# Unread matmuls from the first microsecond, k^T v copied by DMA, and seven taps of a convolution moved to ScalarE under a newly searched order

## The chip, the cores and the metric

The kernel runs on one core of a Trainium2 chip. A time is the device time of one execution in microseconds (us). A profile gives the span of one execution, some 2 us shorter than its time (203.0 against 204.8 us for the kernel before). Engine names: PE is TensorE's matmuls, PEld its weight loads, DVE is VectorE, ACT is ScalarE, POOL is GpSimd, SP is SyncE, which here issues most of the stores.

Some executions of half of the versions here ran some 4 us longer with a recorded PE clock near 0.98 of full. Where a few tenths of a microsecond matter I use only executions with a recorded clock of 0.994 or more, and call them full-clock runs; where all executions of a version are listed, the others are named. The recorded clock doesn't count time before the clock first rises (experiment 4), so a full-clock run can still have had a slow start.

## The reference, cut to what matters

Attention without a softmax, normalized per head, then a feed-forward layer with a gate from a convolution along the sequence. Eight batches, eight heads, 576 positions, head size 64; 512 model columns, 1024 inner columns; fp32 in and out.

```python
kv  = einsum('bhsd,bhse->bhde', k, v)            # 64 x 64 for each head
o   = einsum('bhsd,bhde->bhse', q, kv)
x   = o / sqrt(mean(o*o, axis=-1) + 1e-6) * g    # then heads side by side: 576 x 512
h   = maximum(x @ w_in, 0)                       # 576 x 1024
c   = sum_k conv_w[k] * shift(h, k - 1)          # three taps per column
out = (h * (1 / (1 + exp(-c)))) @ w_out          # 576 x 512
```

## The kernel before

The batches go in five groups (1, 1, 2, 2, 2). The program first lists some 700 operations, each a handful of instructions (a block of matmuls, an eviction, a store), and then sends them out in the sequence of a string that an offline search wrote. A letter after a number is the engine (`a` ScalarE, `d` VectorE), and `*n` puts n unread matmuls, called fillers below, in front of the operation:

```python
ORDER = """
    0 105 11 104 8 10 12 1 2 7 17 18a 9 19 20d 29 30a 24 25d 26*5 27 21 22 6 34 35d 31 32 103 23a 36
    37d 41*7 28d 38*3 40d 33d 4 42 43*6 44 108 109d 39 49 45 46 5 50 3 13 118*9 123 124a 51 53 119a
    106 107a 54 204 47 110*5 111 113 114a ...                                   # cut
"""

def fill(op, ps):                                # the unread matmuls
    for _ in range(op.fill):
        n = min(ps.shape[-1], 288)
        nc.tensor.matmul(ps[:, :n], ident, spread.rearrange("p c m -> p (c m)")[:, :n],
                         start=True, stop=True)
```

k^T v of two heads lands in one PSUM tile, one head on partitions 0 to 63, the other on 64 to 127. The product with q needs each on both halves of the partitions, so for seven of the eight batches it is evicted four times, each time half the partitions (`kv_out`). For the very first batch PE computes it twice (`kv_twice`).

```python
for i in range(2):
    for half in range(2):
        move(st["op"], dst[half * D:(half + 1) * D, :, i, :],
             src[i * D:(i + 1) * D, :, 0, :])
```

The outer taps of the convolution are multiplications of a tile by a column of weights, all on VectorE (`eng` could only be GpSimd otherwise), and output tiles have three buffers:

```python
eng.tensor_scalar_mul(cst["t"][:, f - f0, :], g.h[:, f, lo:lo + T], cw_rel[:, j, f:f + 1])
...
outp = pool("outp", 3)
```

For the last two groups the inverse norms go to DRAM and come back spread over partitions by eight DMAs, all in one operation of the order (`scatter`), issued on SP like the output stores.

Of the kernel before, what the change touches and what calls it, by code (L numbers as in the profile page):

```python
# [25 lines left out]
def _patch_pnc_remap() -> None:  # L26
# [45 lines left out]
KV_TWICE = (1, 0, 0, 0, 0)  # L72
TAPS = ("DVE",)
# [3 lines left out]
    0 105 11 104 8 10 12 1 2 7 17 18a 9 19 20d 29 30a 24 25d 26*5 27 21 22 6 34 35d 31 32 103 23a 36  # L77
    37d 41*7 28d 38*3 40d 33d 4 42 43*6 44 108 109d 39 49 45 46 5 50 3 13 118*9 123 124a 51 53 119a
    106 107a 54 204 47 110*5 111 113 114a 52 48 55 125 112d 56a 126 127d 14 203 202 68 69d 120 122d
    210 211d 121 220 115 116 59 117d 60d 128 129 130 57 58 77 64 207 215 65a 78a 73 74a 221d 131 132  # L80
    61 216d 62 225 226a 133 134 137 208 209a 138 206 135 82 136 83d 205 66 67 212 213 217 232 218
    364 214d 219d 233d 247 139 140a 222 224d 223 248d 227 237 238a 143 144a 242 243d 147 149 63 141
    75 228 142a 148 230 231d 362 79 229a 76 80 81 145 146a 363 15 234 249 250 236d 370 251a 70 239*4
    16 235 71 150 151 367 240 152 371d 153 155 86*3 87a 378 382 366 383d 244 245 156 365 72 379d 167
    252 168d 241d 253 254 374*2 375d 246a 84*3 85 163 164a 169 170a 88 165 154 89 255 157 158 166a
    171 90 259 256 368 369a 173 260 172 160 91 265 175 266 372 373 92d 93 267 268 174 376 377 388
    389a 384 385 396 397a 176 261*2 269 159 100 101a 161 179 516 515 270 262 177 257 386 380 97 387a
    381 390 392 258 178 283 180 393a 391 514 181 185 98d 400 401d 263 394 395 182 183 162 522 523d
    94 264 402 403 526 527d 184 519 398 271 399 95d 99 534 535a 520 521a 186 199 272d 284d 404 405
    285 286d 200a 277 273 278d 274d 287 275 276d 540 548 279 541a 290 549a 280d 518 281 552 528 282a  # L90
    529 517 536 537 538 539a 288 317 318a 309 313 314a 289 310a 291 292 294 293 96 311 312a 305 306a
    295 296 544 545a 550 551 303 304a 102 297 406 315 316a 307 308a 323 546 553d 554 555 547 319 321
    322 530 531a 190 191a 192 542 320 543 524 525 324 328 325 532 533 193 194a 407 408 409 410 556
    557 558 559 413 411 414 196 415 412 416 417 421 422 300 298 301 187 299 419 418 201 420 423 437
    424a 197a 438a 429 430a 431 425 432a 327 326 329 302 195 332 427 198 426a 439 428a 433 434a 441
    440 435 560 436a 442 443 444 445 447 446 331 333 461 462a 465 459 466a 448 460a 330 334 463 455
    456a 467 468a 469 188a 470a 457 458a 189 449 356 357a 358 464a 450 350 351a 352 453 359 360a 361
    563 561 573 471 474 473 341 342a 343 472 475 476 562 574 564 452 335 336a 344 345a 353 354a 480
    477 479 478 481 565 567 568 571 572 566 337 347 338 451 575 576 485 482 569 570 484 577 578a 454
    603 604a 483 486 585 579 580a 586 583 584a 588 607 629 348a 630a 581 582a 601 602a 587 346 511  # L100
    349 512a 608a 355 589 339a 590 591 592 593 605 606a 627 594 595 628a 599 597 625 609 663 496 631
    340 610 613 612 611 614 616 618 664a 598 626a 632a 617 490 497a 615 596 491a 513 498 619 622 620
    505 506a 507 600 633 634 492 636 635 649 651 508 652a 623 637 638 642 640 621 509a 510 641 502
    650a 503a 639 643 647 645 646 624 499 500a 672 690 653 654 644 655 504 501 691a 692 656 658 657
    659 673a 648 493 494a 495 487 665 666 660 667 668 669 661 488a 662 674 675 489 676 677 678 684
    685a 670 671 679 681 682a 687 686 680 693 683 688a 689 694d 695 705 706a 707 696 697d 698 699
    700d 701 702 703a 704
# [23 lines left out]
class Op:  # L131
# [4 lines left out]
    def __init__(self, at, group, engines, cost, fn, args, deps, need, lead, dma, lat):  # L136
        self.at, self.group, self.engines, self.cost = at, group, engines, cost
        self.fn, self.args, self.lead, self.dma, self.lat = fn, args, lead, dma, lat
        self.kind = fn.__name__ if fn else ""
        self.shape = SHAPE.get(self.kind, "")  # L140
        self.deps = sorted({d.at for d in deps})
        self.need = sorted({d.at for d in need})
        self.takes, self.gives = [], []
        self.engine, self.fill = engines[0], 0
# [7 lines left out]
class Plan:  # L152
# [8 lines left out]
    LOADED = 14.4  # L161
# [4 lines left out]
    def op(self, engines, cost, fn, *args, deps=(), need=(), lead=None, dma=0.0, lat=0.0):  # L166
        engines = engines if isinstance(engines, tuple) else (engines,)
        cost = cost if isinstance(cost, tuple) else (cost,) * len(engines)
        o = Op(len(self.ops), self.group, engines, cost, fn, args, deps, need,
               max(cost) if lead is None else lead, dma, lat)  # L170
        self.ops.append(o)
        return o
# [18 lines left out]
def kernel(  # L191
# [37 lines left out]
    nc.scalar.preload_act_table_set(NORM_TABLES)  # L229

# [60 lines left out]
    nc.vector.tensor_copy(spread, spread_ps)  # L291

# [46 lines left out]
    def fill(op, ps):  # L339

        for _ in range(op.fill):
            n = min(ps.shape[-1], 288)
            nc.tensor.matmul(ps[:, :n], ident, spread.rearrange("p c m -> p (c m)")[:, :n],  # L343
                             start=True, stop=True)

    def product(g, bi, t, op):
# [3 lines left out]
        for i in range(2):  # L350
            for e in range(2):
                es = slice(e * D, (e + 1) * D)
                nc.tensor.matmul(  # L353
                    ps[i * D:(i + 1) * D, e, :HS],
                    g.kv[bi][es, t, i, :], g.qT[bi][es, 2 * t + i, :], start=True, stop=True)
# [4 lines left out]
    def attention(g):  # L360
# [3 lines left out]
        for bi, b in enumerate(g.bs):  # L364
            kv_done, free_k, free_q = [], [], []
            outs, tr_done, trs = [], None, []
            for h0, hs in parts(b):
                st = {}

                def kv_mm(bi=bi, b=b, h0=h0, st=st, n=hs // 2):  # L370
                    k_sb, v_sb = qkv["k", b], qkv["v", b]
                    halves = 2 if g.kv_twice else 1
                    st["ps"] = ps = one_bank([P, n, halves, D], FP32, "kv_ps")
                    fill(st["mm"], ps.rearrange("p n i d -> p (n i d)"))
                    for hp in range(n):
                        for i in range(2):
                            h = h0 + 2 * hp + i
                            for r in range(R):
                                for half in range(2) if g.kv_twice else (i,):
# [6 lines left out]
                def kv_out(bi=bi, h0=h0, st=st, n=hs // 2):  # L386
                    if h0 == 0:

                        g.kv[bi] = attn.tile([P, n_hd, 2, D], BF16, name="kv_sb", bufs=6)
                    dst, src = g.kv[bi][:, h0 // 2:h0 // 2 + n, :, :], st["ps"]  # L390
                    if g.kv_twice:
# [7 lines left out]
                if g.kv_twice:  # L399
                    cost, costs = 1.58 * hs / H, (act(hs * 64), dve(hs * 64, 1))  # L400
                else:
                    cost, costs = 0.79 * hs / H, (4 * act(hs * 32), 4 * act(hs * 32) + 0.16)
# [5 lines left out]
                free_k.append(mm)  # L408
                if g.by_dma:
# [9 lines left out]
                for t in range(h0 // 2, (h0 + hs) // 2):  # L419
# [52 lines left out]
                    kps.append(kp)  # L472
                    Hold(TWO, om, [sq, kp])
# [9 lines left out]
        for h0, hs in (parts(0) if first else [(0, H)]):  # L483
            normalize(g, first, range(h0 // 2, (h0 + hs) // 2), sums)
# [7 lines left out]
        elif g.x_from == "dma":  # L492
            Hold(ring("rb", 1), g.scatter, g.x_ops)
        Hold(ring("rs", 1), g.new_rs, g.free_rs)

    def normalize(g, first, ts, sums):
# [81 lines left out]
        if g.x_from == "dma":  # L578
            def scatter():
                scr = dram.tile([P, HS], FP32, name="scr")  # L580
                nc.sync.dma_start(out=scr, in_=g.rs)
                g.rb = big.tile([P, n_hd, 2 * g.G, HS], FP32, name="rb", tag="rb", bufs=1,
                                padded_shape=[P, n_hd, 4, HS])
                for t in range(n_hd):
                    row = scr[t * SM:t * SM + 4 * g.G, :].rearrange("(c i) n -> i c n", i=2)
                    for i in range(2):
                        nc.sync.dma_start(
                            out=g.rb[i * D:(i + 1) * D, t, :, :],
                            in_=row[i:i + 1].to_broadcast([D, 2 * g.G, HS]))

            g.scatter = sp = plan.op("SP", 8.3, scatter, lead=2.5, deps=[rs], need=g.need_rb,
                                     dma=5.3 * g.G, lat=1.0)
            g.free_rs = [sp]
        elif not first:
# [7 lines left out]
        for bi in range(g.G):  # L602
# [8 lines left out]
            for unit in units:  # L611
# [40 lines left out]
                need = []  # L652
                if g.x_from != "keep":
# [8 lines left out]
                if g.x_from == "keep":  # L662
                    xm = plan.op("DVE", 0.46 if len(unit) == 1 else 0.75, x_mul,
                                 deps=need + g.x_of[0][:1])
                else:
                    xm = plan.op("DVE", 0.81, x_scale, deps=need + g.x_of[0][:1])
# [6 lines left out]
    def ffn(g):  # L673
# [15 lines left out]
        for t0, n in units:  # L689
# [30 lines left out]
            so = plan.op("SP", 0.6 * cuts, o_store, deps=[ev], dma=1.2, lat=1.5)  # L720
# [6 lines left out]
    def ffn_steps(g, bis, steps):  # L727
# [3 lines left out]
        for nf, on_pe in steps:  # L731
# [3 lines left out]
            for f in range(f0, f0 + nf):  # L735
                relu = []
                for bi in bis:
# [13 lines left out]
                    def h_out(f=f, bi=bi, st=st):  # L751
# [10 lines left out]
                        g.x_of[bi][:-1] if g.n == 0 else g.x_of[bi]) + [loaded["w_in", f // 4]], need=g.need_h)  # L762
# [42 lines left out]
                def tap(j, f=f, f0=f0, nf=nf, cst=cst):  # L805
                    shape = dict(padded_shape=[P, NF, 2 * S])
                    if f == f0 and j == 0:
                        cst["t"] = conv.tile([P, nf, T], BF16, name="tap", bufs=1, **shape)
                    eng = nc.gpsimd if cst[j, f].engine == "POOL" else nc.vector
                    eng.tensor_scalar_mul(  # L810
                        cst["t"][:, f - f0, :], g.h[:, f, lo:lo + T], cw_rel[:, j, f:f + 1])
# [39 lines left out]
            t_cost = 0.215 + T * 0.00026  # L851
            a_cost = 0.3 + n * 0.00052
            r_tap, r_c = ring("tap", 1), ring("conv", 2)
            t0 = []
            for tap, f, relu in taps:
                cst[0, f] = op = plan.op(TAPS, (t_cost, 2.3 * t_cost)[:1 if TAPS == "DVE" else 2], tap, 0,
# [5 lines left out]
            for tap, f, _ in taps:  # L862
                cst[2, f] = op = plan.op(TAPS, (t_cost, 2.3 * t_cost)[:1 if TAPS == "DVE" else 2], tap, 2,
# [170 lines left out]
```

## Time and profile before

| | kernel before |
|---|---|
| time, median of three runs (lowest to highest) | 206.81 us (204.71 to 209.03) |
| profiled span | 203.0 us |
| PE / DVE / ACT busy | 183.1 / 156.7 / 139.2 us |
| first product with w_in starts, by the chain of waits | 27.98 us |
| last matmul ends | 198.87 us |
| PE idle between these two | 7.6 us |

The table divides the span into three pieces that the whole text uses: the **start** (up to the first product with w_in), the **body** (to the end of the last matmul) and the **tail** (last eviction and store).

### The profile page before, as it was taken

The page shows a single profiled execution, that of the slowest core. Times are in us where ns is not written, and L with a number is a line of the kernel's source. Part 1 is how long each engine was busy: PE and PEld are TensorE (multiplying, and loading weights), DVE is VectorE, ACT ScalarE, POOL GpSimd, SP SyncE. Part 2 cuts the span into 40 slices and gives each one's busy share as a digit, 9 for nine tenths or more (in the row PEclk, how much of TensorE's full clock was granted, in tenths as well). Part 3 has the DMA queues.
Part 4 walks back from the last instruction along what each step waited for, and adds up shares of the span by engine and source line. Part 5 has one row for each costly group of instructions (what it writes and reads, how often), then busy time and mean ns, then how long its engine had stood idle before and what let it go on. Part 6 is the DMA issues. An engine that isn't in the chain of part 4 may idle for free.

```text
span 203.0 us, 4614 instructions
## 1 busy us (share of the span) xinstructions
PE 183.1 (90%) x1854; PEld 115.8 (57%) x1866; DVE 156.7 (77%) x289; ACT 139.2 (69%) x223; POOL 39.9 (20%) x61
## 2 busy tenths in 40 slices
PE   1299998999999999998999998896999999999991
PEld 0275765767677445786754576742447665554440
DVE  2147938677989898588979999999859999998320
ACT  2036474877889888856788969973598598787311
POOL 7706040160400504001001895000000000000000
PEclk9999999999999999999999999999999999999999
DMA  4999999999999699996995010897510341455554
GB/s 53 200 202 203 205 205 204 204 203 204 206 204 204 89 222 187 161 238 153 215 179 145 17 52 29 200 215 207 159 49 3 103 105 52 128 133 157 154 129 130
DMA packets 31593, 31.01 MB, mean 153 GB/s; under 512 B 2108, under 2 KB 26964, under 8 KB 31572
## 3 DMA queue, kind: packets, MB, share of 16 engines
q0 software_dynamic: 20976, 16.25, 52.7%
q1 hardware_dynamic: 10596, 14.47, 28.3%
q8 instruction: 14, 0.23, 0.4%
q14 instruction: 7, 0.06, 0.1%
HBM read 37.24 MB, written 9.73 MB: 231 GB/s over the span
## 4 chain that ended last, share of the span: by engine, by line
PE 52%; DMA 18%; issue 10%; POOL 9%; ACT 5%; DVE 4%; SPq 0%; POOLq 0%; ACTq 0%; DVEq 0%
PE o_ps L698 19%; PE h_ps L746 16%; DMA k_sb<-in_k_dram 7%; DMA out_dram<-o_sb 5%; DMA v_sb<-in_v_dram 3%; PE kv_ps L380 3%; PE qT_ps L430 3%; POOL rs L537 2%; PE rb_ps L624 2%; DMA rb<-scr 2%; PE c_ps L785 2%; ACT sq L453 2%; DVE o L337 2%; PE ot_ps L343 1%; POOL tmp L534 1%
## 5 line engine op out<-in xcount | busy, mean ns | idle before, releaser
L746 PE MATMUL h_ps<-xT,w_in_sb 128*128 128x288 bf16 x512 | 67.4, 286 | 2.2 <-ACT h L757 1.8
L698 PE MATMUL o_ps<-w_out_sb,h 128*128 128x512 bf16 x260 | 60.3, 379 | 2.6 <-ACT o_sb L333 2.0
L746 PEld LDWEIGHTS <-w_in_sb 128*128 128x128 bf16 x512 | 48.9, 98 | 16.5 <-issue 2.9
L698 PEld LDWEIGHTS <-h 128*128 128x128 bf16 x272 | 25.8, 98 | 32.3 <-issue 3.6
L757 ACT ACTIVATE h<-h_ps 128x576 bf16<-128x576 f32 x53 | 33.3, 650 | 9.1 <-PE h_ps L746 8.7
L837 ACT ACTIVATE conv<-conv,cw_rel 128x576 bf16<-128x576 bf16 (+1 forms) x40 | 37.0, 960 | 1.8 <-DVE conv L833 1.6
L810 DVE TENSOR_SCALAR tap<-h,cw_rel 128x576 bf16<-128x576 bf16 (+1 forms) x80 | 31.4, 434 | 2.9 <-ACT h L757 2.1
L333 ACT ACTIVATE o_sb<-o_ps 128x512 f32<-128x512 f32 x30 | 17.8, 593 | 19.8 <-PE o_ps L698 10.3
L453 ACT ACTIVATE sq<-ot_ps 128x576 bf16<-128x576 f32 x32 | 19.9, 652 | 6.9 <-DVE o L337 4.1
L822 POOL COPY conv<-h 128x4 bf16<-128x4 bf16 (+3 forms) x12 | 3.3, 278 | 102.4 <-ACT h L757 71.9
L833 DVE TENSOR_TENSOR conv<-conv,tap 128x1152 bf16<-128x1152 bf16 (+11 forms) x36 | 21.9, 663 | 1.1
L842 DVE TENSOR_TENSOR h<-h,conv 128x1152 bf16<-128x1152 bf16 (+3 forms) x16 | 21.9, 1368 | 1.1 <-ACT conv L837 1.0
L831 DVE TENSOR_TENSOR conv<-h,tap 128x1152 bf16<-128x1152 bf16 (+11 forms) x36 | 20.4, 621 | 0.4
L333 ACT ACTIVATE kv_sb<-kv_ps 64x256 bf16<-64x256 f32 (+1 forms) x25 | 9.6, 383 | 12.2 <-PE kv_ps L380 11.8
L648 DVE SCALAR_TENSOR_TENSOR xT<-ot_ps,g_sb,rb 128x576 bf16<-128x576 f32 x16 | 12.2, 811 | 3.0 <-PE ot_ps L353 2.7
L335 DVE COPY qT<-qT_ps 128x576 bf16<-128x576 bf16 x18 | 8.1, 453 | 8.0 <-PE qT_ps L430 8.0
L642 DVE TENSOR_TENSOR xT<-o,rb_ps 128x576 bf16<-128x576 f32 x15 | 11.0, 750 | 3.7 <-PE rb_ps L627 2.3
L239 POOL DMA_DIRECT2D q_sb<-in_q_dram x9 | 6.9, 770 | 34.9 <-PE qT_ps L430 24.3
L353 PE MATMUL ot_ps<-qT,kv_sb 64*64 64x288 bf16 x192 | 12.7, 306 | 1.0 <-DVE o L337 0.4
L430 PE MATMUL qT_ps<-ident,q_sb 96*128 96x96 bf16 x192 | 13.3, 213 | 0.0
L337 DVE TENSOR_SCALAR o<-ot_ps,g_sb 128x576 f32<-128x576 f32 x12 | 9.6, 813 | 4.9 <-ACT sq L453 4.1
L380 PE MATMUL kv_ps<-v_sb,k_sb 96*64 96x64 bf16 x432 | 9.9, 204 | 3.4 <-DMA v_sb<-in_v_dram 2.7
(73 smaller groups left out, 160.5 us busy)
## 6 DMA issues: line engine op xcount, KB each, us to landing
out_dram<-o_sb SPq DMA_DIRECT2D x24, 192.0 KB, 2.3
rb<-scr SPq DMA_DIRECT2D x16, 288.0 KB, 6.1
q_sb<-in_q_dram POOLq DMA_DIRECT2D x7, 576.0 KB, 8.5
v_sb<-in_v_dram POOLq DMA_DIRECT2D x7, 576.0 KB, 11.9
k_sb<-in_k_dram POOLq DMA_DIRECT2D x7, 576.0 KB, 14.2
out_dram<-o_sb SPq DMA_DIRECT2D x24, 128.0 KB, 2.4
out_dram<-o_sb SPq DMA_DIRECT2D x24, 64.0 KB, 2.0
w_in_sb<-in_moe_w_in_dram POOLq DMA_DIRECT2D x2, 512.0 KB, 14.9
```

The costliest lines, as they stand in the source:

```text
L333: nc.scalar.activation(dst, src, AX.Copy, scale=1.0 if scale is None else scale)
L380: nc.tensor.matmul(ps[half * D:(half + 1) * D, hp, i * (halves - 1), :], k_sb[:, h, r * D:(r + 1) * D], v_sb[:, h, r * D:(r + 1) * D], sta ...
L430: nc.tensor.transpose(ps[:, i, j * PS:(j + 1) * PS], q_sb[:, 2 * t + i, j * P:(j + 1) * P], ident[:PS, :PS])
L453: nc.scalar.activation(g.sq[bi, t], ust["ps"][:, :, :HS], AX.Square)
L698: nc.tensor.matmul(st["ps"][:n, :], g.h[:, f, t0:t0 + n], w_out_sb[:, f, :], start=(f == 0), stop=(f == n_ff - 1))
L746: nc.tensor.matmul(ps[:, e, :HS], w_in_sb[:, t, f * P:(f + 1) * P], g.xT[:, t, at:at + HS], start=(t == 0), stop=(t == n_hd - 1))
L757: nc.scalar.activation(dst, st["ps"][:, :, :HS], AX.Relu)
L810: eng.tensor_scalar_mul(cst["t"][:, f - f0, :], g.h[:, f, lo:lo + T], cw_rel[:, j, f:f + 1])
L831: nc.vector.tensor_add(c[:, :, here], h[:, :, here], t[:, :, there])
L833: nc.vector.tensor_add(c[:, :, there], c[:, :, there], t[:, :, here])
L837: nc.scalar.activation(cst["c"][:, f - f0, :], cst["c"][:, f - f0, :], AX.Sigmoid, scale=cw_rel[:, 1, f:f + 1])
L842: nc.vector.tensor_mul(hs, hs, cst["c"])
```

## The change

Four things at once. A tile of ones is set at the very start, so that unread matmuls can run from about the first microsecond, before any load lands, and not only from the time when identity and spread matrix exist. k^T v is evicted once, and two DMAs copy its halves across the partitions. Taps may go to ScalarE. And the search wrote a new order, in which the spreading of the norms is four separate operations, so that stores can go between them. The intent is a full PE clock at the first real matmul, less eviction work on ScalarE, and less waiting in the body.

```diff
-KV_TWICE = (1, 0, 0, 0, 0)
-TAPS = ("DVE",)
+KV_FROM = ("twice", "swap", "swap", "swap", "swap")
+TAPS = ("DVE", "ACT")
 ORDER = """            # all of it is new; cut
-    0 105 11 104 8 10 12 1 2 7 17 18a 9 19 20d 29 30a 24 25d 26*5 27 21 22 6 34 35d 31 32 103 23a 36
+    103 8 11 0 7 17*7 18d 9 19*6 20a 24 21*2 29 25d 26 104 22 30d 27 31*4 32 12 10 34*1 35d 36*1 23a
@@ start of the program
+    ones = consts.tile([P, 288], BF16, name="ones")
+    nc.vector.memset(ones, 1.0)
+    warm_ps = ps_one.tile([P, 288], FP32, name="warm_ps", tag="one")
+    def warm(n):
+        for _ in range(n):
+            nc.tensor.matmul(warm_ps, ones[:, :P], ones, start=True, stop=True)
+    warm(14)
@@ after the spread matrix
     nc.vector.tensor_copy(spread, spread_ps)
+    warm(22)
@@ fill
-            nc.tensor.matmul(ps[:, :n], ident, spread.rearrange("p c m -> p (c m)")[:, :n],
+            nc.tensor.matmul(ps[:, :n], ones[:, :P], ones[:, :n],
@@ kv_out
+                    if g.kv_from == "swap":
+                        g.kv[bi] = attn.tile([P, 2, n_hd, D], BF16, name="kv_sb", bufs=6)
+                        move(st["op"], g.kv[bi][:, 0, :, :], st["ps"][:, :, 0, :])
+                        return
@@ new operation on SP
+                def kv_swap(bi=bi):
+                    for i in range(2):
+                        nc.sync.dma_start(out=g.kv[bi][(1 - i) * D:(2 - i) * D, 1, :, :],
+                                          in_=g.kv[bi][i * D:(i + 1) * D, 0, :, :])
@@ norms: one operation "scatter" becomes one write and four reads
-                for t in range(n_hd):
+            def gather(t):
 ...
@@ tap
+                    if cst[j, f].engine == "ACT":
+                        nc.scalar.activation(dst, src, AX.Copy, scale=cw_rel[:, j, f:f + 1])
+                    else:
+                        nc.vector.tensor_scalar_mul(dst, src, cw_rel[:, j, f:f + 1])
```

Left out as well: the product with q reads k^T v from its new place. The rest of the diff is the planner's cost figures, dependencies and bookkeeping.

## The prediction

> **What bounds the kernel now.** I read, in this order: busy times of the page, the two stretches of the span before and after the first product with w_in, the PE waits, the order of the start, and the landing times of the first loads.
>
> ```profile
> PE 183.1 (90%) x1854; PEld 115.8 (57%) x1866; DVE 156.7 (77%) x289; ACT 139.2 (69%) x223; POOL 39.9 (20%) x61
> ```
>
> ```profile
> 9.00:28.00 19.00, 19.00 (x273) 12.93 (x274) 11.81 (x24) 9.06 (x18) 3.85 (x5) 1.00 1.30 204
> 28.00:199.00 171.00, 163.24 (x1566) 102.19 (x1576) 142.74 (x249) 128.31 (x205) 28.89 (x41) 1.00 0.77 150
> ```
>
> The columns of the stretches are length, busy PE, PEld, DVE, ACT, POOL, PE clock, DMA share, GB/s. PE is occupied for all of 9 to 28 us and for 163.2 of 171 us after it, so PE's own queue sets the end: 9.0 us before the first load lands, 19.0 us of start, 171 us of body (7.8 us of it idle), 4.1 us for the last eviction and store (the last matmul ends at 198.9, the span at 203.0). What can be won is only: PE work that goes, PE work that was slow, and the 7.8 us.
>
> The start is less full than it looks:
>
> ```profile
> 9.00 2.13 PE L380 MATMUL kv_ps<-v_sb,k_sb 96*64 96x64 bf16 x72 [2.72 <-DMA v_sb<-in_v_dram]
> ...
> 11.07 1.85 PE L430 MATMUL qT_ps<-ident,q_sb 96*128 96x96 bf16 x18
> ...
> 12.72 1.40 PE L343 MATMUL ot_ps<-spread,ident 128*128 128x288 bf16 x5
> ...
> 15.67 1.02 PE L343 MATMUL ss_ps<-spread,ident 128*128 128x288 bf16 x7
> ```
>
> L343 are matmuls whose result nobody reads; they fill waits to keep PE warm. By the chain of waits five of them took 1.20 us (240 ns each) at 12.9 us and seven took 0.86 us (123 ns each) at 15.8: PE runs at half speed from 9.0 to about 14 us. The page's clock row reads 1.00 there, so it does not show this. There are 49 such matmuls, 35 of them before 28 us (some 4.9 us of its 19) and 14 after.
>
> ```profile
> w_in_sb<-in_moe_w_in_dram POOLq DMA_DIRECT2D x1, 512.0 KB, 16.1
> k_sb<-in_k_dram POOLq DMA_DIRECT2D x1, 432.0 KB, 5.3
> v_sb<-in_v_dram POOLq DMA_DIRECT2D x1, 432.0 KB, 6.7
> q_sb<-in_q_dram POOLq DMA_DIRECT2D x1, 432.0 KB, 7.9
> ```
>
> Issue times (1.29, 2.22, 3.08, and 9.15 for w_in) plus these landings: k at 6.6, v at 8.9, q at 11.0, the first half of w_in at 25.25. The start has two floors set by loads: no transpose of q before 11.0, no product with w_in before 25.25. The first such product now starts at 27.8.
>
> The body's idle time, by the waits of PE:
>
> ```profile
> PE o_ps L698 <- ACT o_sb L333: 2.0, 1, 2.0
> PE h_ps L746 <- ACT h L757: 1.8, 2, 1.1
> ...
> PE kv_ps L380 <- DMA k_sb<-in_k_dram: 0.7, 1, 0.7
> PE ss_ps L507 <- ACT sq L453: 0.6, 1, 0.6
> ```
>
> ```profile
> 120.00:130.00 10.00, 8.23 (x67) 6.29 (x66) 9.93 (x13) 8.98 (x12) 4.29 (x4) 1.00 0.28 74
> 130.00:140.00 10.00, 9.94 (x64) 5.17 (x63) 9.86 (x13) 6.59 (x10) 0.22 (x1) 1.00 1.08 241
> 140.00:150.00 10.00, 7.95 (x46) 3.57 (x47) 8.88 (x14) 6.10 (x8) 0.00 (x0) 1.00 0.40 122
> ```
>
> From 110 to 140 us DVE is full too (9.66, 9.93, 9.86 of 10 us): there DVE and PE bound together. The 2.0 us wait at 142 is an output buffer not yet stored, because the store stood on SP behind the broadcast of the norms, which waited for GpSimd's Newton steps (110.8 to 124.1 us).
>
> **What the Trainium skill says.** "TensorE: Matmul & The Clock Gate", Part 1: the PE clock is halved until it has been busy for a window of about 3.4 us, which runs freely. The trace agrees: 240 against 123 ns, the change about 5 us after the first dense work. "ScalarE: Activation LUTs", Rules for kernel authors: about 0.3 us per instruction plus 0.83 ns per element. For ACT from SBUF the trace gives (1247-769)/576 = 0.83 ns and 0.29 us. "DMA: Bandwidth & Descriptors", Queues, rings and completion order: all queues share the same engines, which alternate between them by packet. The trace: a 192 KB store takes 2.3 us in the quiet end, 5.8 us between 60 and 70 us beside the loads. "Perfetto Trace Analysis", Identifying the Most-Contended Engine, counsels to distrust busy PE; 8 of the 379 ns output matmuls take 1.73 us in the chain, so durations of single matmuls must not be added up, and I use the chain's.
>
> **The change by parts.** The order string lists operations by number, with the engine and the count of unread matmuls; I numbered the operations of both programs as the code makes them and compared.
>
> 1. Warm-up. 14 unread matmuls go out as soon as a tile of ones is set (about 1.3 us), 22 more after the spread matrix, 7 in front of the first k^T v and 6 in front of the first transpose. Estimate: 14 x 240 ns end at 4.7, the 16 small transposes (0.62) at 5.3; warm about 5 us after the beginning, so about 5 cold (1.1 us) and 17 warm (2.1 us) reach 8.5, and 7 more (0.85) end at 9.4. The first k^T v (72 at 20 ns, as 48 take 0.96) ends at 10.8 instead of 11.1. q lands at 11.0, and six fillers reach beyond that: the transposes start at about 11.4, as now. The cold k^T v was hidden behind q. The gain comes after it: now 11.1 to 27.98 is 16.9 us. After: transposes 1.4 (four at 0.36), products 1.0, second k^T v 0.5, sums of squares 0.7, fp32 broadcasts 4 x 1.16 = 4.6, k^T v of batch 1 1.0, its transposes 1.3, the tap matrix 0.3, 27 fillers 3.3: 14.1 us. So w_in begins at 25.5, just past its landing. **Gain 2.4 us**; there is no more without an earlier w_in.
>
> 2. k^T v by DMA. Seven batches had four evictions each (24 on ACT at 378 ns, 4 on DVE at 421) and get one each, plus two DMAs of 32 KB on SP. About 9.1 us leave ACT and 1.7 us leave DVE; some 2.3 and 0.4 come back (estimates from the same rows; partitions don't count). PE's work is the same.
>
> 3. Taps and other placements. 7 of 80 taps go to ACT: four of 576 (0.365 to 0.769 us), three of 1152 (0.537 to 1.247). Evictions of h on DVE go from 11 to 18, the kept products there from 12 to 8, the output evictions there from 6 to 3. Sums: DVE -1.7 +0.4 -3.1 +5.3 -3.3 -2.1, and +0.5 for the first batch's first k^T v: about -4, to 153. ACT -9.1 +2.3 +6.8 -4.6 +3.0 +1.8 -0.5: about 0, to 139. Freed ACT time is spent on relieving DVE by 2.5%. Neither was the bound over the whole span, and PE's sum of products is unchanged, so this part is worth only what it takes from the 7.8 us.
>
> 4. The new order, with broadcasts split by tile and stores placed between them. There are 57 fillers in waits, 17 of them after the start (2.1 us, against 14, 1.7 us, now): the search itself expects PE to wait in the body as much as before. From the order, the store stuck on SP should be freed, since 13 to 15 us of PE work lie between the Newton steps and the broadcast; that wait (2.0) and part of the two on h (1.8) may go. Others will come in their place, as DVE stays as full. I put the idle at 5.5 instead of 7.8 us, and 0.4 more fillers: **gain 1.9 us**.
>
> Sum: 2.4 + 1.9 = 4.3 us, span 198.7. On the median of 206.8 that is 202.5.
>
> **Rivals.** (a) The copy by DMA is late. Its 64 rows of 512 bytes share the engines with the loads, which run at 204 GB/s until 65 us; loaded transfers took 4 to 7 us. For it: an in-order PE stands still at the first product. Against: the new order puts about 7 us of other PE work between eviction and use. If each of the first four copies were 1 us late: 204 to 206, within 2%. (b) The start gains nothing, as DVE and ACT (11.8 and 9.1 us of 19) or the landing of w_in hold it. The landing allows 2.5 us at most, the chain of evictions between norms and x is mostly fillers, which marks waits. Time then 205. (c) DVE is the bound from 60 to 150 us and decides: 4 us less work in it gives up to 4 us, not 1.9; then 200 to 201.
>
> **Range and chances.** 2% of 206.8 is 4.1 us, just under my sum, so it is nearly an even call. Runs of before differ by 4.3 us among themselves, against which fast runs alone are steadier. I lean to faster since both repairs (clock, stuck store) are visible waits and the search was fitted to this trace; slower would need rival (a) at every batch. Range 198.5 to 205.7.
>
> **What would show it.** Right: unread matmuls from about 1.3 us, all at 122 ns after about 7; transposes at 11.2 to 11.4; first w_in product at 25.3 to 25.8; ACT busy near 139 and DVE near 153; PE idle in the body near 5.5 us, no wait for output buffers over 1 us. Wrong: PE waits for the copies of kv (products after a DMA), unread matmuls running past 9.5 us and delaying k^T v, first w_in product still after 27, or body idle of 8 us or more under a new name.

## More of the kernel before

The prediction shows the busy times, the stretches, the loads and PE's waits. One more view helps, the chain of waits at the end of the start. It is followed back from the last instruction; columns are start, length, and what occupied that time.

```profile
26.66 0.72 PE ot_ps L343 x5
27.38 0.25 PE ot_ps L353 x4
27.62 0.36 PE qT_ps L430 x6
27.98 0.61 PE h_ps L746 x5
```

Everything in it is PE, including the five unread matmuls of L343: PE's own queue, not another engine, delays the first product here.

## The result, and the profile after

The changed kernel took 199.85, 199.91, 200.16 and 204.06 us; the last ran with a recorded clock of 0.982. The median is 200.03 us, beside 206.35 us for four runs of the kernel before. Ratios are computed as the mean time of one kernel's fast runs over that of the other's of the same rounds, so they are not quite the ratio of these medians: 0.972, with a 95% interval of 0.964 to 0.980. The change is faster by 2.8%. The prediction was 202.5, with 198.5 to 205.7 as the range.

The busy times and the stretches, which answer to the lines that the prediction shows (the first two stretches are now cut exactly at the first product with w_in and at the end of the last matmul):

```profile
PE 188.7 (95%) x1910; PEld 118.1 (60%) x1910; DVE 153.2 (77%) x281; ACT 139.2 (70%) x211; POOL 40.6 (21%) x61
```

```profile
9.00:26.85 17.85, 17.41 (x270) 10.96 (x269) 10.53 (x25) 7.76 (x14) 3.84 (x5) 1.00 1.30 204
26.85:193.20 166.35, 163.54 (x1586) 101.91 (x1583) 140.61 (x242) 129.55 (x196) 29.60 (x41) 1.00 0.79 158
120.00:130.00 10.00, 10.00 (x75) 7.29 (x75) 9.73 (x11) 7.91 (x13) 3.94 (x3) 1.00 0.25 73
130.00:140.00 10.00, 10.00 (x66) 4.54 (x65) 9.61 (x15) 8.51 (x11) 0.51 (x1) 1.00 0.98 259
140.00:150.00 10.00, 10.00 (x71) 5.74 (x70) 9.43 (x13) 8.40 (x11) 0.00 (x0) 1.00 0.51 133
```

Columns as in the prediction: length, then busy PE, PEld, DVE, ACT and POOL, the PE clock, the DMA share, GB/s. PE is occupied without a gap in the three stretches where it had lost 3.9 of 30 us, while DVE is about as full there as it was. Over the body PE is idle for 166.35 - 163.54 = 2.8 us; before it was 170.89 - 163.25 = 7.6 us. The second figure is a little high: the trace of before holds only 260 of the 272 output matmuls (all 272 weight loads are there), and the same work with all records present is 164.0 us in experiment 2, which would make it 6.9. The lengths of the pieces don't depend on this:

| piece | before | after | difference |
|---|---|---|---|
| start, to the first product with w_in | 27.98 | 26.85 | -1.13 |
| body, to the end of the last matmul | 170.89 | 166.35 | -4.54 |
| tail, to the end of the span | 4.13 | 4.80 | +0.67 |
| span | 203.0 | 198.0 | -5.0 |

The start on PE, by the timeline (start, length, instructions; in square brackets the idle time before and what ended it):

```profile
1.23 6.64 PE L242 MATMUL warm_ps<-ones 128*128 128x288 bf16 x36 [1.23 <-DVE eps_sb L290]
...
9.10 1.33 PE L397 MATMUL kv_ps<-v_sb,k_sb 96*64 96x64 bf16 x72
10.36 0.91 PE L359 MATMUL qT_ps<-ones 128*128 128x288 bf16 x6
...
16.79 1.23 PE L660 MATMUL rb_ps<-rs,spread 32*128 32x288 f32 x4
```

All 36 unread matmuls go out in one row, and it shows when the clock rises: up to 5.28 us they start some 240 ns apart, from 5.5 us on some 123 ns apart, and the clock record kept in the trace begins at 5.46 us. The first k^T v takes 1.33 us where it took 2.13: PE is at full speed from the first load on. The end of the start, by the chain of waits, shows a new piece that was not in the chain before:

```profile
25.19 1.20 ACT qT L349 x2
...
26.44 0.41 PE qT_ps L460 x6
26.85 1.96 PE h_ps L785 x16
```

PE's waits after (total us, how often, longest), with the first line the 1.2 us before the tile of ones exists:

```profile
PE warm_ps L242 <- DVE eps_sb L290: 1.2, 1, 1.2
PE ot_ps L371 <- ACT qT L349: 0.6, 2, 0.4
PE ot_ps L371 <- DVE h L798: 0.5, 1, 0.5
...
PE ot_ps L371 <- DMA kv_sb<-kv_sb: 0.3, 1, 0.3
```

The wait of 2.0 us for an output buffer and the 1.8 us on h evicted by ACT are gone. On SP, stores now go out between the reads of the norms (first line before, the others after):

```profile
125.95 5.26 SPq L587 DMA_DIRECT2D rb<-scr  x8
127.46 2.62 SPq L620 DMA_DIRECT2D rb<-scr  x4
130.18 1.20 SPq L751 DMA_DIRECT2D out_dram<-o_sb  x2
131.42 1.31 SPq L620 DMA_DIRECT2D rb<-scr  x2
```

The new copies make PE wait once, for 0.3 us, although they took 3.5 us at best, 5.2 in the median and 6.4 at worst from issue to landing.

### The profile page after: what moved, and what is told of

It is laid out like the page before. It is cut to its first block, busy times and chain, and to the rows that moved or that the text cites. A ratio compares the mean times of both kernels' runs of the same rounds, so it can differ in the third digit from the quotient of the medians.

```text
span 198.0 us, 4714 instructions
## 1 busy us (share of the span) xinstructions
PE 188.7 (95%) x1910; PEld 118.1 (60%) x1910; DVE 153.2 (77%) x281; ACT 139.2 (70%) x211; POOL 40.6 (21%) x61
## 4 chain that ended last, share of the span: by engine, by line
PE 74%; DMA 9%; DVE 8%; ACT 5%; issue 1%; POOL 0%; SPq 0%; DVEq 0%; ACTq 0%
PE o_ps L737 27%; PE h_ps L785 24%; DMA v_sb<-in_v_dram 6%; PE warm_ps L242 3%; PE ot_ps L371 3%; DMA kv_sb<-kv_sb 3%; PE qT_ps L460 3%; PE kv_ps L397 2%; PE c_ps L825 2%; PE rb_ps L660 2%; PE o_ps L928 2%; DVE tap L853 2%; ACT qT L349 2%; DVE h L884 2%; DVE conv L875 1%; DVE conv L873 1%
## 5 line engine op out<-in xcount | busy, mean ns | idle before, releaser
L737 PE MATMUL o_ps<-w_out_sb,h 128*128 128x512 bf16 x272 | 61.4, 379 | 0.0
L796 ACT ACTIVATE h<-h_ps 128x576 bf16<-128x576 f32 x46 | 28.9, 649 | 8.3 <-PE h_ps L785 8.2
L853 DVE TENSOR_SCALAR tap<-h,cw_rel 128x576 bf16<-128x576 bf16 (+1 forms) x73 | 29.7, 449 | 2.4 <-ACT h L796 1.3
L349 ACT ACTIVATE o_sb<-o_ps 128x512 f32<-128x512 f32 x33 | 19.7, 597 | 15.4 <-PE o_ps L737 10.3
L875 DVE TENSOR_TENSOR conv<-conv,tap 128x1152 bf16<-128x1152 bf16 (+11 forms) x36 | 20.4, 622 | 1.1
L349 ACT ACTIVATE qT<-qT_ps 128x576 bf16<-128x576 bf16 x14 | 8.8, 649 | 15.8 <-PE qT_ps L460 15.8
L798 DVE TENSOR_SCALAR h<-h_ps 128x576 bf16<-128x576 f32 x18 | 13.3, 753 | 5.4 <-PE o_ps L928 2.7
L460 PE MATMUL qT_ps<-ident,q_sb 96*128 96x96 bf16 x192 | 12.6, 206 | 0.1
L460 PEld LDWEIGHTS <-q_sb 96*128 96x128 bf16 x192 | 10.5, 97 | 2.5 <-issue 0.8
L371 PEld LDWEIGHTS <-kv_sb 64*64 64x64 bf16 x192 | 5.0, 104 | 9.3 <-issue 7.6
## 6 DMA issues: line engine op xcount, KB each, us to landing
k_sb<-in_k_dram POOLq DMA_DIRECT2D x7, 576.0 KB, 11.4
```

The source lines that it names most:

```text
L349: nc.scalar.activation(dst, src, AX.Copy, scale=1.0 if scale is None else scale)
L371: nc.tensor.matmul(ps[i * D:(i + 1) * D, e, :HS], kv, g.qT[bi][es, 2 * t + i, :], start=True, stop=True)
L460: nc.tensor.transpose(ps[:, i, j * PS:(j + 1) * PS], q_sb[:, 2 * t + i, j * P:(j + 1) * P], ident[:PS, :PS])
L737: nc.tensor.matmul(st["ps"][:n, :], g.h[:, f, t0:t0 + n], w_out_sb[:, f, :], start=(f == 0), stop=(f == n_ff - 1))
L796: nc.scalar.activation(dst, st["ps"][:, :, :HS], AX.Relu)
L853: nc.vector.tensor_scalar_mul(dst, src, cw_rel[:, j, f:f + 1])
```

## The experiments

Twelve kernels ran, all correct, on two chips, beside new runs of the kernel before. On the first chip (eight of them) the four full-clock runs of the kernel before took 204.33, 205.37, 205.45 and 206.14 us, mean 205.3; its others took 206.93 to 209.27 at clocks of 0.981 to 0.992. "The warm-up" below is the early row of unread matmuls. What follows compares means of full-clock runs with each other, two to nine a side.

### 1. The changed kernel once more

> The changed kernel itself, as the ground for the other runs on this chip. Theory: 199.8 to 200.3, with now and then a run of 204 in which the granted clock drops in the middle. Rival (the chip differs from that of the first result): all runs shifted by more than 0.5.

No edit. 200.18, 200.07, 200.80 and 200.05 us, all at full clock, mean 200.3; the ratio to the kernel before is 0.974 (0.958 to 0.990), so these rounds alone would not settle 2%. In its profile the first product with w_in starts at 27.01 and PE's last matmul ends at 193.62. So between two traces of one kernel the start moves by 0.16 us and the body by 0.26 us; the differences in the table above are well beyond that.

### 2. The kernel before with the warm-up alone

```diff
+    warm(14)                  # at the start, with the tile of ones
 ...
     nc.vector.tensor_copy(spread, spread_ps)
+    warm(29)
```

> The kernel before with 43 unread matmuls on a tile of ones ahead of the first loads, nothing else. Without a warm-up, two kernels gave 202 in some executions and 212 to 217 in others, with matmuls at half speed until 37 us; and before itself scatters from 204.7 to 209.3. Theory (before pays for a PE that warms at a moment that differs from run to run, 14 us in its profiled run): the scatter goes, all runs without a clock drop within 0.4 of one another, at 203.0 to 203.6, 1.3 to 1.8 below the best run of before and some 3 below its mean; first product with w_in at 26.3 to 26.8 instead of 27.8. Rival 1 (the start is held by loads and evictions): 204.5 to 205, first product at 27.5 or later, though the scatter may go. Rival 2 (the scatter of before has another cause, in its body): scatter of over 2 us stays.

202.97, 203.61, 202.86, 204.07 and 202.88 us at full clock, mean 203.3, and 203.98 at 0.992: 2.0 us below the kernel before. In the profile the first product with w_in starts at 26.96, 1.0 us earlier, and the body is 170.07 us, 0.8 shorter: the wait for the output buffer shrank from 2.0 to 0.7 us, without anything in that part of the program having been touched, while one for a load of k grew from 0.7 to 1.2.

```profile
PE h_ps L757 <- ACT h L768: 1.8, 2, 1.1
...
PE o_ps L709 <- ACT o_sb L344: 0.7, 1, 0.7
```

So the warm-up moves the start by about 1 us, in the old order as in the new one. The rest of its 2.0 us came through waits that shifted later on.

### 3. The same, with a fourth output buffer

```diff
-    outp = pool("outp", 3)
+    outp = pool("outp", 4)    # on top of 2
```

> Before with the warm-up and a fourth output buffer. In the trace of before PE stood for 2.0 us at 142 us since no output buffer was free while its store waited on SP behind the broadcast. Theory (that wait is on the path that sets the end, and part of the new order's gain is its removal): 1.2 to 2.0 us below the same kernel with three buffers, the 2.0 us wait gone from the list. Rival (DVE is full there and PE would wait for it a little later): less than 0.5 us, and another wait of PE of over 1 us between 140 and 160 us.

202.18, 202.47 and 201.25 us at full clock, mean 202.0 (one more, 205.85, at 0.981). The wait for the output buffer is gone from the list, and the body is 169.3 us. 1.3 us for one buffer is more than the 0.7 us of the wait; three runs that spread by 1.2 us do not settle more than the sign. It does show that part of what the new order gained could have been had in the old one.

### 4. The changed kernel without the warm-up

```diff
-    warm(14)
-    warm(22)
-    17*7 ... 19*6             # fillers before the first k^T v and the first transposes
+    17 ... 19
```

> The changed kernel without the 36 warm-up matmuls and without the 13 unread ones in front of the first k^T v and the first transpose. Theory (a warm clock is worth what the start gained, 1.1 us): the first product with w_in moves from 26.85 to 28.0 to 28.4 us, the time from 200.0 to 201.1 to 201.5. Rival 1 (the start is held by loads and by evictions, the clock is worth nothing): first product at 26.9 to 27.2, time 200.0 to 200.3. Rival 2 (the whole 2.4 us of my prediction were lost clock, and other things took 1.3 back): first product at 29.2 or later, time 202.4 or more.

201.78, 202.43 and 201.90 us, and 211.84 for the execution that was profiled, all with a recorded clock of 0.994 or more. The mean of the three is 202.0: the warm-up is worth 1.8 us when the kernel is lucky. The fourth shows what it also does. The stretch from the first k^T v to the first product with w_in, one block of that time, and that product itself:

```profile
9.00:37.30 28.30, 28.25 (x261) 15.90 (x261) 10.64 (x24) 7.74 (x14) 3.85 (x5) 1.00 1.22 191
```

```profile
19.76 2.28 PE L652 MATMUL rb_ps<-rs,spread 32*128 32x288 f32 x4
...
37.13 3.40 PE L777 MATMUL h_ps<-xT,w_in_sb 128*128 128x288 bf16 x16
```

The four fp32 broadcasts took 2.28 us where they take 1.23 in the changed kernel, and the first sixteen products 3.40 instead of 2.12. PE was occupied for 28.25 of 28.3 us and stayed at half speed all the way; only the dense 128 by 128 products after 37 us brought it up. The clock column reads 1.00 throughout, since the trace's clock record begins only at 39.72 us; in this phase the clock must be read from durations. Experiment 6 shows the same in three executions out of four.

### 5. The kernel before without its fillers at the start

```diff
-    26*5 ... 41*7 ... 38*3 ... 43*6 ... 118*9 ... 110*5
+    26   ... 41   ... 38   ... 43   ... 118   ... 110
```

> Before without the 35 unread matmuls of its start (the 14 of the body stay), no warm-up either. The changed kernel without its warm-up kept PE occupied without a break from 11 to 39 us at half speed in one of four executions,[...] and cost 212; the same with the parts undone 214 in two of four. Theory (the dense unread matmuls at 12.7 to 18.6 us are what raises the clock of before; occupied PE alone does not): at least half of the executions stay at half speed past 30 us, first product with w_in at 33 us or later, 211 or more. Rival (they only fill waits; the useful work raises the clock within about 5 us as it did in the profile of before): first product at 27 to 28.5, 204 to 206.5 in all executions without a clock drop.

208.51, 208.02 and 208.04 us on the second chip, beside nine full-clock runs of the kernel before from 205.19 to 206.69 there; ratio 1.010 (1.004 to 1.015). Taking 4.9 us of work out of PE's full queue made the kernel 2 us slower:

```profile
31.33 2.12 PE L746 MATMUL h_ps<-xT,w_in_sb 128*128 128x288 bf16 x8
...
36.33 1.15 PE L746 MATMUL h_ps<-xT,w_in_sb 128*128 128x288 bf16 x8
```

The first eight products start at 31.33 us instead of about 28 and take 2.12 us, against 1.15 for the same block five microseconds later. The clock record begins at 34.54 us, against 14.59 in the kernel before. The fillers of the kernel before bought a full clock at the price of their own time. This is why PE's occupied start was not proof of useful work.

### 6. The new order alone

```diff
-    all of the warm-up; one eviction and two DMAs; seven taps on ScalarE
+    nothing; four evictions; all taps on VectorE, in the changed kernel's order
```

> All three parts undone together (no warm-up, four evictions, all taps on DVE), so only the new order with its other placements and the split of the broadcasts remain. Theory: the losses add, 203 to 205, so the order by itself is worth 1 to 3 us against before. Rival 1 (the order alone made the body shorter): 201.2 to 201.8, only the warm-up missing. Rival 2 (the order is worth nothing without the parts it was searched for): 205.5 or more, as before.

203.09 us once, and 213.73, 213.96 and 216.80 us: the cold start of experiment 4, in three of four executions. There is no verdict on the order from this run, except that it depends on the warm-up. It has 27 fillers between the first transposes and the first product with w_in, where the old order has 35; that the search could spend fewer because PE is warm when it gets there is a guess.

### 7. The warm-up and the new order, without copy and taps

```diff
-    one eviction and two DMAs; seven taps on ScalarE
+    four evictions; all taps on VectorE
```

> The changed kernel with its warm-up kept, but four evictions per batch and all taps on DVE: the new order alone, warm. Measured apart, the evictions gave 201.5 and the taps 201.4 (same kind of runs), 1.5 and 1.4 above 200.0. Theory (the order was fitted to both; their losses add at different places): 202.4 to 203.2, so that order alone is worth 0 to 1 us against before with a warm-up. Rival 1 (one engine is eased by undoing the taps, ACT, and so takes the four evictions for free): 201.0 to 201.6. Rival 2 (they multiply): over 203.5.

201.49 and 201.29 us at full clock, mean 201.4 (two more, 203.55 and 205.32, at 0.989 and 0.979). Against the old order with the warm-up (203.3) the new order is worth 1.9 us, though this rests on two runs. The split reads of the norms and the other moved evictions are part of it and were not tested apart. Copy and taps together then give 201.4 - 200.3 = 1.1 us. A rival is left: the order was searched for with copy and taps in it, so undoing them may cost because it no longer fits, and no order was searched without them.

### 8. The changed kernel with four evictions again

```diff
-    move(st["op"], g.kv[bi][:, 0, :, :], st["ps"][:, :, 0, :])
+    for i in range(2):
+        for half in range(2):
+            move(st["op"], g.kv[bi][half * D:(half + 1) * D, int(i != half), :, :],
+                 st["ps"][i * D:(i + 1) * D, :, 0, :])
 ...
-    the two copying DMAs
```

> The changed kernel with four evictions per batch again in place of one and two copies by DMA; same order, so six times 4 x 0.378 instead of 0.384 us on ACT and once on DVE: about 8 us more work for the two, none for PE. Theory (the copy pays by the ACT time it frees, which the order spends elsewhere): PE idles 1.5 to 3 us more in the body, time 201.5 to 203. Rival 1 (the gain of the body is the order alone, ACT has slack): time within 0.4 of 200.0. Rival 2 (the copy is what gained the body's 4.5 us): 204 or more.

200.91, 201.49, 201.70 and 201.65 us at full clock, mean 201.4: 1.2 us lost. ACT is busy for 145.5 us, 6.3 more, but the first product with w_in starts at 26.91 us, as in the changed kernel, and PE waits in the body:

```profile
PE h_ps L786 <- ACT h L797: 1.2, 3, 0.5
PE rb_ps L359 <- DVE xT L679: 0.8, 1, 0.8
```

These two lines are not among the waits of the changed kernel. PE's last matmul ends at 194.39, so the body is 1.1 us longer; that is the whole loss.

### 9. The changed kernel with all taps on VectorE

```diff
-    148a 150a 175a 450a 456a 489a 601a
+    148d 150d 175d 450d 456d 489d 601d
```

> The changed kernel with its seven ACT taps back on DVE at the same places: DVE +3.1 us, ACT -6.8 us, in stages where DVE is busy 9.3 to 9.8 of 10 us. Theory (DVE bounds beside PE between 100 and 160 us; three of the taps lie before 60 us and are free there): half of it comes back, time 200.6 to 201.6. Rival (taps are placed where either engine has slack): 199.8 to 200.3, possibly less, as a tap takes half as long on DVE.

201.59 and 201.30 us at full clock, mean 201.4, and 204.42 (0.980, the profiled one) and 204.13 (0.983). Undoing the taps alone costs 1.2 us, undoing the evictions alone costs 1.2 us, and undoing both (experiment 7) costs 1.1 us. The two parts do not add up: each pays only together with the other. My reading, which no run shows: the freed ACT time is what takes the taps, and the lighter DVE is of use only if ACT doesn't become the late one instead.

Its profile fell on one of the 0.98 executions and shows what this one is:

```profile
71.00:71.50 0.50, 0.00 (x0) 0.00 (x0) 0.50 (x1) 0.17 (x1) 0.00 (x0) 1.00 1.32 204
...
72.00:73.00 1.00, 1.00 (x40) 0.98 (x35) 0.00 (x0) 0.00 (x0) 0.00 (x0) 0.50 1.29 209
```

PE waited for one load of v, 0.99 us; then the clock column fell to 0.50, stayed there to about 78 us and came back (the 2 us from 78 on read 0.88). The profiles of experiments 6 and 7, also near 0.98, have one such loss each, at the same place of the order. So at least in these three the slower execution is not a slower chip but one loss of the clock in the body; of the others only the mean clock is known. This part of the order is thin for PE (short broadcasts between fillers). The changed kernel's profile, at full clock, is idle for 0.3 us between 70 and 72 us where this one is idle for 1.0. That the wait brought the fall about is likely, not proved: in the 3.4 us before the fall PE was idle for 1.0, 1.1 and 0.8 us in experiments 9, 7 and 6, but experiment 12 waited 0.77 us at this place and kept the clock, and so did the kernel before in its 2.0 us wait at 142 us. The length of a wait alone doesn't decide.

### 10. The copy in the old order

```diff
-    four evictions            # on top of 2, order of the kernel before
+    one eviction, and the two DMAs issued right behind it
```

> Before with the warm-up, and with one eviction and two copies by DMA per batch in place of four evictions, in the old order, where the first product often follows the evictions at once (kv at 24.5 us, its use at 27.3; 41.0 and 43.0; 50.6 and 52.4; 66.3 and 68.3). In the trace after, a copy landed 3.5 to 6.4 us after its issue, 5.2 in the median. Theory (the copy pays only in an order that leaves this time between): PE stands for a copy two to four us in each of the first four batches, 6 to 12 us in all, against 203.3 of before with the warm-up: 208 to 214. Rival 1 (copies land in some 2 us when issued early, ACT time saved counts): 202 to 203.3. Rival 2 (half of it is hidden by other waits that go): 204 to 207.

223.21 to 225.31 us, ratio 1.085 (1.079 to 1.092): slower by 8.5%, far more than expected. Against 203.3 us for experiment 2 that is some 21 us, of which PE's waits in two lines are 14.7:

```profile
PE ot_ps L365 <- DMA kv_sb<-kv_sb: 9.9, 6, 4.1
PE ot_ps L365 <- DVE xT L665: 4.8, 2, 4.4
```

```profile
50.00:52.00 2.00, 0.00 (x0) 0.00 (x0) 0.00 (x0) 0.00 (x0) 0.00 (x0) 1.00 1.29 205
52.00:54.00 2.00, 1.69 (x17) 1.05 (x18) 0.23 (x1) 0.91 (x2) 0.00 (x0) 0.67 1.32 203
54.00:56.00 2.00, 2.00 (x13) 1.21 (x10) 1.68 (x3) 0.28 (x1) 0.00 (x0) 0.50 1.31 204
```

The copies did not land later than in the changed kernel (1.7, 3.3 and 5.9 us at least, median and most, against 3.5, 5.2 and 6.4). They were needed earlier. For batch 1 in both, a copy landed about 4.9 us after its issue; the changed kernel issues it at 22.2 and first uses it at 28.7 us, the old order issues it at 24.9 and asks for it at 27.0. Each long wait is paid again after it, as the second block shows: after 4.1 us of idling, up to 52.24, PE runs at half clock for about 3.5 us. The clock record has four such stretches, from 25.4, 52.7, 83.4 and 134.6 us, 23.9 us in all. The second line of waits, on x, I have not traced. Not every loss of the clock has that cause: near 26 us the column was already at 0.50 while PE was occupied for 2.00 of 2.00 us, ahead of the wait; it had not been idle in the 3.4 us before the fall.

### 11. One eviction before the first product moved to VectorE

```diff
-    115a ... 46
+         ... 46 115d          # a transpose of batch 1 evicted by VectorE, later
```

> The changed kernel with one of the four evictions of batch 1's transposes moved from ACT to DVE, after the third product of x. In its trace PE waits 1.2 us at 25.2 us, since four evictions of 0.65 us queue on ACT while the transposes behind them have no PSUM bank; my prediction had counted no such wait, and the first product with w_in came at 26.85 instead of 25.5. Theory (this wait is the missing part of the start's gain): first product at 26.1 to 26.4, time 199.4 to 199.8 against 200.1 of the changed kernel on this chip. Rival 1 (the last x product, at 26.0 to 26.5 us, holds the first product whatever the transposes do): first product at 26.6 or later, 199.9 to 200.3. Rival 2 (the start shortens but the loads hold the body): first product early, time the same.

199.48 to 200.59 us, mean 200.1, on the second chip: no gain. No run of the changed kernel is recorded as on that chip; in ratios to the kernel before, 0.970 stands beside its 0.972. The 1.20 us on ACT is gone from the chain, and another piece stands in its place:

```profile
25.40 0.69 PE rb_ps L660 x2
...
26.12 0.45 DVE xT L671
26.57 2.16 DVE diag L966 x2
```

By the timeline the first product with w_in now starts at 26.53 us, just when the last quarter of x is there; in the two traces of the changed kernel it starts at 26.69 and 26.85 by the same view. The two waits stood side by side; taking one away moved the start by 0.2 to 0.3 us, which the time doesn't show.

### 12. All small repairs together

```diff
+    11; four output buffers; 19*2 instead of 19*6; the product of the narrow tails one place earlier
```

> An attempt at a better kernel: the changed one with the moved eviction, two unread matmuls instead of six ahead of the first transpose (they ran to 11.27 us, q had landed at 10.9), four output buffers, and the last narrow product one place earlier, so that a product of full width ends the kernel. Theory: 0.5 us from the eviction, 0.3 from the fillers, 0.2 to 0.5 from the end (4.8 us between the last matmul and the end of the span, 4.1 in before), none from the buffers: 198.8 to 199.5. Rival (PE's work bounds the body and what the start gains is lost to loads or DVE): 199.7 to 200.2.

200.01, 200.13, 199.81, 199.62 and 200.08 us at full clock (203.44 at 0.983), ratio 0.970 (0.966 to 0.974): the same as the changed kernel. The tail is 4.6 us instead of 4.8. I found no version that beats the changed kernel.

## Why the prediction was right or wrong

The call (faster, just above 2%) and the range held, and both things it rested on, PE's clock at the start and the stuck store in the body, are seen in the profiles. But both terms of the sum were mis-sized in opposite directions, and a third was missing: -2.4 and -1.9 were predicted, -1.1, -4.5 and +0.7 came. That the span came so close, 198.0 us for 198.7, is luck: the errors nearly cancel. The rest of the distance from 202.5 to 200.03 us is in the base, a median of 206.8 us over three executions of which one took 209.03. Full-clock means on one chip give the parts: 205.3 before, 203.3 with the warm-up, 201.4 with the new order, 200.3 with copy and taps.

**The start, right in mechanism, 1.3 us too large.** The unread matmuls start at 1.23 us (predicted about 1.3), with the 16 transposes of the spread matrix behind the whole row, at 7.80 us, and not in its middle. They overrun the landing of v (issued at 2.22, landed 6.5 us later, at 8.7) by some 0.4 us, and leave PE at full speed; the transposes start at 11.27 by the chain (predicted 11.2 to 11.4). The step that failed is "14.1 us" from there to the first product; it took 15.6. By the chain after 11.27 us these 15.6 us are 8.65 of PE's own work without fillers (predicted 10.8; the rest runs beside evictions), 3.69 of fillers (predicted 3.3) and 3.24 of evictions on ACT and DVE with their issue, of which my sum had none. It added PE's work in a row, as if PE never had to wait for its own PSUM tiles; in the chain before that was nearly so: it is PE alone, with fillers ahead of many steps. My reading is that they covered such waits and a shorter PE queue uncovered them. Four evictions of 0.65 us queue on ACT at its end, and experiment 11 shows the last part of x standing just behind them. Rival (b), which let DVE and ACT hold the start, was therefore half right.

**The body, right in mechanism, 2.6 us too small.** I read 17 fillers after the start as a sign that the search itself expected as much waiting as before, and put the idle time at 5.5 us. It is 2.8. The number of fillers was no measure of the waits that remain. The two waits that I named did go (2.0 and 1.8 us), and fewer came in their place than I allowed for, although DVE is as full between 120 and 150 us as it was. Experiment 2 shows a part of this that I had not thought of: the warm-up alone made the body of the old order 0.8 us shorter.

**The copy by DMA.** Busy times came out as computed (ACT 139.2, DVE 153.2 against 139 and 153). Rival (a), late copies, costs 0.3 us here, for the reason given: some 6 us of other work lie between issue and use. Experiment 10 is that rival made real, and it is far worse than the "204 to 206, within 2%" that I gave it: the waits were up to 4.1 us, not 1, and a long wait also costs the clock. The prediction called part 3 "worth only what it takes from the 7.8 us". The trace of experiment 8 agrees, as all of its loss lies in the body; those of 7 and 9 fell on slow executions and cannot say. Experiments 7 to 9 show a gain only for copy and taps as a pair. Rival (c), DVE as the bound, named the time that came (200 to 201), but the runs don't bear out its reason: experiment 7 has 3.9 of the 5.0 us, and DVE is busy for 156.7 us in it, exactly as in the kernel before.

**The tail** was taken as unchanged and became 0.67 us longer. The last product is now that of the narrow tails, whose two stores of 128 KB are issued one after the other. In experiment 12, which moves it one place earlier, the tail is 0.2 us shorter again; the rest I have not traced.

**Still open.** The moment at which the clock rises within the early row differs: in the ten traces with a warm-up the record begins between 4.50 and 7.08 us, which is 3.3 to 5.9 us after the first unread matmul. With the latest two (experiments 9 and 7, 6.80 and 7.08 us) the row itself runs longer at half speed, the first k^T v starts at 9.75 and 9.89 instead of 9.10 us, and the first product with w_in at 27.50 and 27.64 instead of 26.85. In all fourteen traces the stretches between two changes of the clock are whole multiples of 3.41 us (19, 2 and 36 times in experiment 9), but what sets the moment is not shown, nor which property of the later work keeps an early clock up. The order's own 1.9 us rests on two full-clock runs on one side.

## What to carry to other kernels

Where the first load takes several microseconds to land, fill that time with dense matmuls on a constant tile: it costs little on a path that waits for the load anyway, as long as the row isn't so long that a late rise of the clock carries it past the landing, and no start with it stayed at half speed here. When PE's queue is emptied at one place, look for the evictions that its padding had covered, and do not add up PE's work alone. A copy by DMA instead of evictions pays only if the order puts more work between issue and use than the copy takes in the loaded machine, here about 6 us.

## What the Trainium skill lacked or had wrong

- "TensorE: Matmul & The Clock Gate", Part 1, What's actually happening, on three points. It says that the clock rises after about 3.4 us of sustained busy PE; here PE was occupied for 28.25 of 28.3 us and stayed at half speed (experiment 4), with k^T v of 64 columns, fp32 broadcasts from 32 rows, transposes and 27 fillers in groups of at most four as its work. Part 4 says that transposes don't count as busy in the same way; of the other forms the page doesn't say which count. It puts the ramp at less than 1% of a typical span; without the warm-up it cost 10 us of 202 (about 5%) in one of four executions of experiment 4 and some 11 us in three of four of experiment 6, while no execution of a kernel with the warm-up, experiment 10 left aside, took more than 205.9 us. And it gives an idle window of about 3.4 us for the fall to half clock: in experiment 9 the clock fell right after 0.99 us of idling in a thin stretch and stayed at 0.50 for 6.8 us, and in experiment 10 it fell once while PE was occupied. The fall after 4.1 us of idling there fits the section.
- "DMA: Bandwidth & Descriptors", Anatomy of one DMA, gives about 2 us of fixed time per transfer and bytes over 436 GB/s, measured on another path. Copies of 32 KB within SBUF took 3.5 to 6.4 us in the changed kernel, the first beside loads at about 200 GB/s; the page has no figure for small copies on a loaded machine.
- No page says how the clock column of these profiles reads before the clock first rises. It shows 1.00, while PE runs at half speed and the clock record of the trace has no entry yet: from 9 to 37 us in experiment 4, for instance (2.28 against 1.23 us for the same four matmuls), where the record begins at 39.72 us.
